# Attention scores in two row halves of TensorE, in two steps a pair, and a new order for the first batch

## The chip, the cores and the metric

The kernel runs on one core of a Trainium2 chip. Its time is the device time of one execution, in microseconds (us). A core has TensorE (matmuls, PE in the profile; PEld is its weight loads), VectorE (DVE), ScalarE (ACT), GpSimd (POOL) and SyncE (SP); SP, POOL and ACT also issue DMA transfers, each in its own queue and in program order. Where a profile row says 128*64, the stationary operand of a matmul has 128 rows (the contraction) and 64 columns.

## The reference

Batch 8, 8 heads, 576 tokens, 64 values a head; 8 token indices are global. All of it in fp32, the kernel's matmuls in bf16.

```python
scores = 0.125 * q @ k.T
mask = (|i - j| <= 32) | is_global[i] | is_global[j]
attn = softmax(where(mask, scores, -1e9))
x = (attn @ v), heads side by side          # 4608 tokens x 512
h = x @ w_in                                # 512 x 2048
g = s * relu(h) ** 2 + b
out = g @ w_out                             # 2048 x 512
```

## The kernel before

**Attention.** The 64 (batch, head) are taken as 32 pairs of heads (p = 0 to 31), four pairs a batch. A pair's K and Q are transposed so that head 0 lies on partitions 0 to 63 and head 1 on 64 to 127. Keys come in five chunks of 128 (120 keys and the 8 global ones), queries in a row of 640 columns, with 8 columns of global queries in each chunk. Chunk c needs only the query columns LO[c] to HI[c]: 160, 192, 192, 192 and 136 of them. Scores come out transposed, keys on partitions and queries on columns.

`qbufs` hold Q as a block diagonal, `[128, 2, 640]`: for head 0 the lower partitions are zero, for head 1 the upper, so that one matmul with all 128 rows of a K chunk gives both heads' scores side by side. A pair has five score steps, `qk(p, c)`, one a chunk, of 2 x 160 to 2 x 192 columns. Each takes a tile of `ps_s` (two buffers of one PSUM bank) and ends in an exponential on ScalarE (L583, L586). For pairs 0 to 4 the mask is added by a matmul of `ident` with a bias table (L573, L579); from pair 5 on VectorE multiplies the exponentials with a 0/1 mask at the next step (L587, through the list `later`).

`pvq(m, blk)` makes the weighted sums of two pairs (m): value rows and a column of ones are stationary, 128x32, four heads in four column groups of the array; query columns are cut in two blocks (0 to 323, 324 to 615) over the five chunks. `norm_steps` divides by the sums: logarithm and negative exponential on ScalarE, then sums and scalings on VectorE into `xt`. `scatter` copies the global tokens' columns into `xt` on POOL, at addresses that POOL has read into registers (`greg_p`, L1008).

**Feed-forward.** `moe_quanta` is a generator: per tile of 512 tokens 16 groups of four matmuls with `win_t` (psh, L698), ReLU on ScalarE, square on VectorE, then 16 groups of four with `wout_t` (pso, L732). `Q()` takes one group ("quantum"), `lead()` one of the two leading pieces of tile 0, which need heads 0 and 1 of `xt` alone.

**Order.** All engines follow the program order written by hand. The first batch (`first_pair`, p = 0 to 4) runs by itself: a table says at which score step which transposes, copies and normalising steps come. Its global K and Q columns come by a matmul with a selection matrix for pairs 0 and 1 (`select`), and from a gather by indirect DMA for the others (`gather(0)`, `globals_of(0)`: `round_g`, `turn`, `move`). Then `run_pair` has eight steps (s) a pair, scores in the first five, and a quantum in nearly each. Q transposes of the next pair stand at s = 5 and use a buffer of `ps_s` too. From pair 8 on K is turned by DMA (`turn_k`, after `round_k`). `cast_v` rounds V into `vring`; `put_v` puts the eight global V rows in.

Of the kernel before, what the change touches and what calls it, by code (L numbers as in the profile page):

```python
# [49 lines left out]
STEP = (CUT, 360)  # L50
MASKED = 1.0e9
# [18 lines left out]
def kernel(  # L70
# [29 lines left out]
    ps_s = ctx.enter_context(tc.tile_pool(name="ps_s", bufs=2, space=bass.MemoryType.PSUM))  # L100
# [52 lines left out]
    qbufs = [const.tile([P, 2, LQ], BF16, name=f"qbd{i}", tag=f"qbd{i}") for i in range(3)]  # L153
    gqd = [const.tile([P, 2, D], BF16, name=f"gqd{i}", tag=f"gqd{i}") for i in range(2)]
# [107 lines left out]
    def clear(ap, n):  # L262
        nc.scalar.copy(out=ap, in_=view(zero[0 : ap.shape[0]], [0, n]))

    onesf = const.tile([P, P], FP32)
    nc.vector.memset(onesf[:], 1.0)
    nc.vector.memset(qbufs[0][0:D, 1], 0.0)
    nc.vector.memset(qbufs[0][D:P, 0], 0.0)
    for t in "kq":
        nc.vector.memset(six[t][NP6:P, 0, :, NJ - 2 :], 0.0)  # L270

    nc.sync.dma_start(
# [20 lines left out]
    for p in range(5):  # L293
        load_v(nc.sync, p)
        if p == 0:
            nc.sync.dma_start(out=sbrow[:, 0:1], in_=_bcast_dram(moe_s[:], 1))
            nc.sync.dma_start(out=sbrow[:, 1:2], in_=_bcast_dram(moe_b[:], 1))
# [34 lines left out]
    def gather(bb, ts="kq"):  # L332
# [26 lines left out]
    iot = const.tile([P, WM], FP32)  # L359
    nc.gpsimd.iota(  # L360
        iot[:, 0:GAP], pattern=[[1, GAP]], base=NG - WIN, channel_multiplier=-1,
        allow_small_or_imprecise_dtypes=True,
    )
    nc.gpsimd.iota(
        iot[:, GAP + NG : WM], pattern=[[1, WM - GAP - NG]], base=HB + NG,
        channel_multiplier=-1, allow_small_or_imprecise_dtypes=True,
    )
    nc.gpsimd.memset(iot[:, GAP : GAP + NG], 100000.0)
    gadd = [const.tile([P, WM], FP32, name=f"gadd{i}", tag=f"gadd{i}") for i in range(2)]
    for t in gadd:  # L370
        nc.gpsimd.memset(t[:], -MASKED)
        nc.gpsimd.memset(t[0:NG, WIN : WIN + P], 0.0)
    band = const.tile([P, WM], FP32)

    def halves(t, eng, h):
# [5 lines left out]
    clear(qbufs[1][0:D, 1], LQ)  # L381
    halves("k", nc.scalar.copy, 1)
    halves("q", nc.scalar.copy, 1)
    nc.scalar.activation(band[:], iot[:], AF.Square)
    nc.gpsimd.tensor_scalar(
        out=band[:], in0=band[:], scalar1=(float(WIN) + 0.5) ** 2, scalar2=MASKED,
        op0=OP.is_le, op1=OP.mult,
    )
    masks, biases = [], []

    def build_biases(cs):
        for c in cs:
            at = sum(W[:c])
            m = wsum[:].bitcast(BF16)[:, at : at + W[c]]
            x0 = LO[c] - P * c + WIN
            nc.vector.scalar_tensor_tensor(
                out=m, in0=band[:, x0 : x0 + W[c]], scalar=notg[:, c : c + 1],
                in1=gadd[c // (NCH - 1)][:, x0 : x0 + W[c]], op0=OP.mult, op1=OP.add,
            )
            biases.append(view(m, [0, 2], [1, W[c]]))  # L400

    def build_masks():
        for c in range(NCH):
            at = sum(W[:c])
            m = const.tile([P, W[c]], BF16, name=f"mask{c}", tag=f"mask{c}")
            nc.vector.tensor_scalar(
                out=m[:], in0=wsum[:].bitcast(BF16)[:, at : at + W[c]],
                scalar1=-0.5, scalar2=None, op0=OP.is_ge,
            )
            masks.append(view(m[:], [0, 2], [1, W[c]]))  # L410
# [17 lines left out]
    def globals_of(bb):  # L428
# [11 lines left out]
        def turn():  # L440
# [7 lines left out]
            def evac():  # L448
                eng = nc.vector.tensor_copy
                eng(out=gkt[bb][:], in_=ps[:, 0])  # L450
                for hh in range(2):
                    r = slice(D * hh, D * hh + D)
                    eng(out=gqd[bb % 2][r, hh], in_=ps[r, 1])
# [26 lines left out]
    def put_kq(p):  # L480
        bb, x = divmod(p, 8)
        eng = A if p < 4 else V
        eng(
            out=view(ktile[p], [P, NCH], [1, NG]),
            in_=view(gkt[bb][:, NG * x : NG * x + NG], [0, NCH], [1, NG]),
        )
        eng(  # L487
            out=view(qbufs[p % 3][:, 0, HB:], [LQ, 2], [P, NCH], [1, NG]),
            in_=view(gqd[bb % 2][:, 0, NG * x :], [D, 2], [0, NCH], [1, NG]),
        )  # L490

    def trans(t, p):
        if p < 5 or (t == "k" and p > 5):
            ps = bank("pst").bitcast(BF16)[:, 0:LQ]
        else:
            ps = ps_s.tile([P, LQ], BF16, tag="s", name="pst")
# [22 lines left out]
    def trans_a(p, later=later):  # L519
# [4 lines left out]
        def evac():  # L524
# [4 lines left out]
            if p == 3:  # L529
                r, n = slice(0, D), HB // NJ  # L530
                nc.vector.tensor_copy(
                    out=view(qbufs[p % 3][r, 0], [P, NCH], [HB + NG, 2], [NJ, n], [1, NJ]),
                    in_=view(qtp[0][r], [2 * n, NCH], [n, 2], [1, n], [NP6, NJ]),
                )
            if 1 < p < 6:
                put_kq(p)
# [3 lines left out]
    qtp = [None]  # L540

    def trans_b(p, later=later):
        ps = qtp[0] = trans("q", p)

        def evac():
            n = HB // NJ
            for hh in (1, 0):
                eng = A if (p, hh) in ((0, 1), (0, 0), (1, 1), (2, 1), (3, 1)) else V
                if eng is V and p == 3:
                    continue  # L550
                r = slice(D * hh, D * hh + D)
                if p >= NSIXQ:
                    eng(  # L553
                        out=view(qbufs[p % 3][r, hh], [P, NCH], [HB + NG, 2], [1, HB]),
                        in_=view(ps[r], [P, NCH], [HB, 2], [1, HB]),
                    )
                    continue
# [622 lines left out]
```

## Time and profile before

| | |
|---|---|
| median of 3 runs | 356.03 us (355.75 to 356.8) |
| profiled execution | 356.0 us, span 354.3 us |
| TensorE busy in the span | 329.9 us (93%) |
| VectorE, ScalarE, POOL busy | 232.7, 219.0, 66.0 us |
| mean granted TensorE clock | 0.981 of full |

The span goes from the first to the last instruction. In a timeline each row is one or more instructions of one line that follow each other: start, duration from the first start to the last end, engine, line, operation, output<-inputs, how many; in brackets how long the engine was idle before, and what ended that. Matmuls are pipelined and their recorded ends include the time to come through, so from one matmul's start to the next one's is the better measure; a few matmul records can be missing. A start in a row can be a little earlier than the end of the row before.

### The profile page before, as it was taken

What the parts mean: (1) busy time and instruction counts of PE and PEld (TensorE: products, weight loads), DVE (VectorE), ACT (ScalarE), POOL (GpSimd) and SP (SyncE); (2) the same over time, 40 slices, a digit from 0 to 9 for tenths busy, and PEclk for the clock granted to TensorE, in tenths of its full rate; (3) what the DMA queues carried; (4) which work ended last, traced back from release to release, by engine and by line L of the source; (5) the groups of instructions that cost most, each with busy time, mean ns of one, the idle gap of its engine ahead of it and who ended that gap; (6) DMA issues with size and microseconds to landing.
All of it is one profiled execution on the core that took longest, in us unless ns stands there. A gap on an engine that the chain in (4) does not pass through costs nothing.

```text
span 354.3 us, 8484 instructions
## 1 busy us (share of the span) xinstructions
PE 329.9 (93%) x3131; PEld 174.0 (49%) x3175; DVE 232.7 (66%) x670; ACT 219.0 (62%) x454; POOL 66.0 (19%) x150
## 2 busy tenths in 40 slices
PE   5868499999999999999999999999999999999996
PEld 3434244454455454557755545544557644444444
DVE  5748367877778888876768686767677644423421
ACT  4647367865987588757876787678747713602610
POOL 5863663005000701030005000300020010000000
PEclk9969879999999999999999999999999999999999
DMA  8999998978997799999189967983440011011002
GB/s 155 222 218 217 208 214 149 187 131 192 208 144 160 171 188 226 206 198 172 23 174 242 208 125 164 247 192 79 150 132 2 2 61 60 1 59 62 0 30 91
DMA packets 122246, 50.23 MB, mean 142 GB/s; under 512 B 108992, under 2 KB 115328, under 8 KB 122196
## 3 DMA queue, kind: packets, MB, share of 16 engines
q1 hardware_dynamic: 113530, 37.84, 53.7%
q0 software_dynamic: 8320, 11.42, 16.1%
q10 hardware_dynamic: 354, 0.43, 0.7%
q8 instruction: 25, 0.41, 0.5%
q14 instruction: 17, 0.14, 0.1%
HBM read 42.35 MB, written 9.44 MB: 146 GB/s over the span
## 4 chain that ended last, share of the span: by engine, by line
PE 77%; DMA 7%; DVE 4%; issue 4%; POOL 3%; ACT 2%; POOLq 1%; SPq 1%; ACTq 0%; DVEq 0%
PE psh L698 32%; PE pso L732 30%; PE pss L574 6%; PE po L604 5%; DMA wst<-in_moe_w_out_dram 3%; DMA natq<-in_q_dram 2%; DMA gf<-in_v_dram,grow 2%; PE pst L499 1%; PE pst L513 1%; POOLq L1008 1%; DVE wsum L1055 1%; PE pss L573 1%; DVE qbd L553 1%; POOL sixk L169 1%; DVE g L723 1%
## 5 line engine op out<-in xcount | busy, mean ns | idle before, releaser
L698 PE MATMUL psh<-xt,win_t 128*128 128x512 bf16 (+4 forms) x685 | 137.3, 342 | 5.5 <-POOL xt L675 4.6
L732 PE MATMUL pso<-wout_t,g 128*128 128x512 bf16 (+1 forms) x569 | 132.9, 373 | 2.1 <-issue 1.4
L720 ACT ACTIVATE r<-psh 128x512 bf16<-128x512 f32 x144 | 86.7, 604 | 58.5 <-PE psh L698 51.3
L698 PEld LDWEIGHTS <-win_t 128*128 128x128 bf16 x704 | 64.2, 98 | 60.5 <-issue 7.7
L732 PEld LDWEIGHTS <-g 128*128 128x128 bf16 x592 | 56.0, 98 | 58.6 <-issue 0.5
L586 ACT ACTIVATE e<-pss 128x384 bf16<-128x384 f32 (+2 forms) x135 | 63.1, 471 | 34.8 <-PE pss L574 32.6
L723 DVE TENSOR_TENSOR g<-r 128x512 bf16<-128x512 bf16 x144 | 59.9, 427 | 37.4 <-ACT r L720 36.4
L587 DVE TENSOR_TENSOR em<-e,mask 128x384 bf16<-128x384 bf16 (+2 forms) x135 | 45.7, 339 | 12.8 <-ACT e L586 11.0
L574 PE MATMUL pss<-qbd,kt 128*128 128x384 bf16 (+2 forms) x160 | 51.0, 322 | 3.2 <-DVE qbd L880 1.5
L675 POOL COPY xt<-xg 128x4 bf16 (+1 forms) x72 | 17.9, 249 | 175.4 <-DVE xt L650 171.6
L752 DVE SCALAR_TENSOR_TENSOR osb<-pso,sb,bias_row 128x512 f32<-128x512 f32 (+1 forms) x25 | 18.1, 726 | 29.7 <-PE pso L732 27.0
L574 PEld LDWEIGHTS <-kt 128*128 128x128 bf16 x160 | 15.8, 99 | 20.2 <-DVE qbd L487 2.7
L650 DVE TENSOR_TENSOR xt<-po,rep 128x480 bf16<-128x480 f32 (+2 forms) x60 | 24.4, 446 | 0.3 <-ACT rep L660 0.3
L553 DVE COPY qbd<-pst 64x600 bf16<-64x600 bf16 x38 | 17.8, 467 | 9.2 <-PE pst L499 8.6
L558 DVE COPY qbd<-pst 64x600 bf16<-64x600 bf16 x20 | 15.6, 780 | 9.8 <-PE pst L513 6.4
L583 ACT ACTIVATE em<-pss 128x384 bf16<-128x384 f32 (+2 forms) x25 | 11.3, 461 | 16.6 <-PE pss L574 13.9
L604 PE MATMUL po<-em,vring 128*32 128x160 bf16 (+3 forms) x840 | 17.1, 218 | 1.1 <-issue 1.1
L205 ACT CAST natb<-natk 128x640 bf16<-128x640 f32 x24 | 17.8, 740 | 0.0
L248 ACT CAST vring<-natv 128x640 bf16<-128x640 f32 x21 | 15.6, 743 | 0.0
L657 ACT ACTIVATE ln<-po 128x324 f32<-128x324 f32 (+1 forms) x30 | 13.1, 437 | 3.8 <-PE po L604 3.7
L660 ACT ACTIVATE rep<-ln 128x324 f32<-128x324 f32 (+1 forms) x32 | 15.3, 477 | 0.1
L229 ACT CAST sixq<-natq 120x640 bf16<-120x640 f32 x19 | 14.3, 755 | 0.0
(137 smaller groups left out, 236.0 us busy)
## 6 DMA issues: line engine op xcount, KB each, us to landing
natv<-in_v_dram SPq DMA_DIRECT2D x57, 150.0 KB
natk<-in_k_dram SPq DMA_DIRECT2D x47, 150.0 KB
out_dram<-osb SPq DMA_DIRECT2D x23, 256.0 KB
natq<-in_q_dram SPq DMA_DIRECT2D x37, 150.0 KB
wst<-in_moe_w_out_dram POOLq DMA_DIRECT2D x8, 512.0 KB
out_dram<-osbh SPq DMA_DIRECT2D x9, 256.0 KB
win_t<-in_moe_w_in_dram POOLq DMA_DIRECT2D x4, 512.0 KB
wout_t<-in_moe_w_out_dram POOLq DMA_DIRECT2D x4, 512.0 KB
```

The lines of the kernel that those rows point to most:

```text
L553: eng(out=view(qbufs[p % 3][r, hh], [P, NCH], [HB + NG, 2], [1, HB]), in_=view(ps[r], [P, NCH], [HB, 2], [1, HB]),)
L574: nc.tensor.matmul(ps[:], ktile[p][:, P * c : P * c + P], qbufs[p % 3][:, :, LO[c] : HI[c]], start=p == 0 or p >= NCH, stop=p > 0,)
L586: nc.scalar.activation(e[:], ps[:], AF.Exp, scale=SCALE)
L587: later.append(lambda: nc.vector.tensor_mul(em[:], e[:], masks[c]))
L604: nc.tensor.matmul(po[DH * j : DH * j + DH, a : a + n], view(vring[:, p % NVR, c, hh, part - 1 :], [2, DH]) if part else onesb[:], emt[(p, ...
L650: nc.vector.tensor_tensor(out=view(xt[:, 2 * g, x0 + t0 :], [NXT, 2], [w, runs], [1, w]), in0=view(po[:, STEP[blk] + col :], [STEP[blk], 2 ...
L675: nc.gpsimd.tensor_copy(out=xt[:, h, S * (bi % NX) : S * (bi % NX) + S][:, :, ds(greg_p[i], 1)], in_=xgs[bi][:, h, i : i + 1],)
L698: nc.tensor.matmul(psh[:, d0 : d0 + n], win_t[:, a, f * P : f * P + P], xt[:, a, x0 : x0 + n], start=(a == 0 and j == 0), stop=(a == 3), s ...
L720: nc.scalar.activation(r[:], psh, AF.Relu)
L723: later.append(lambda g=g, r=r: nc.vector.tensor_mul(g[:], r[:], r[:]))
L732: nc.tensor.matmul(pso[:, 0:nn], gl[f][:, u * P : u * P + P], wout_t[:, f, n0 : n0 + nn], start=(f == 0), stop=(f == 15),)
L752: nc.vector.scalar_tensor_tensor(out=osb[:, 0:nn], in0=pso[:, 0:nn], scalar=s_bc, in1=bias_row[:, n0 : n0 + nn], op0=OP.mult, op1=OP.add,)
```

## The change

Q lies plain in `qbufs`, `[128, 640]`, head 0 on the upper and head 1 on the lower 64 partitions; zeros and their clearing go. A score matmul takes one head: 64 rows of K by 128 keys, against that head's query columns; the two heads alternate and write to two PSUM banks of one tile. The five steps become two, `qk(p, g)`, with the chunk pieces (`PIECES`) that fall in one block of the weighted sums: 160 + 192 + 100 = 452 columns a head, and 92 + 192 + 136 = 420. `ps_s` is one buffer of two banks. In `run_pair` the steps stand at s = 0 and 4 of odd pairs and at 1 and 3 of even ones; `put_out`, the weighted sums, stays at s = 4 of odd and 1 of even pairs.

`first_pair` and its tables are replaced by a straight list. Pairs 0 to 3 take their global K and Q columns by `select`; the gather serves V rows and pairs from 4 on. Some copies of V move from ScalarE to VectorE, the mask band is made on POOL, the scatter of the first batch stands ahead of weight loads on POOL, the register reads come earlier, V of pairs 5 and 6 is loaded from SP's queue.

```diff
+PIECES = []
+for _x0, _x1 in SPAN:          # per block: (chunk, lo, hi, offset)
...
-    ps_s = ctx.enter_context(tc.tile_pool(name="ps_s", bufs=2, ...))
+    ps_s = ctx.enter_context(tc.tile_pool(name="ps_s", bufs=1, ...))
...
-    for p in range(5):
+    load_v(nc.sync, 0)              # ahead of three fills of V's buffers
...
+    for p in range(1, 6):
         load_v(nc.sync, p)
...
-    nc.scalar.activation(band[:], iot[:], AF.Square)
-    nc.gpsimd.tensor_scalar(out=band[:], ...)
+    nc.gpsimd.memset(band[:], MASKED)
+        chop(ap, n, 1, b0 + WIN, -1, 0.0)       # affine_select, four and two more
...
     def trans_b(p, later=later):
-            for hh in (1, 0):
-                eng = A if (p, hh) in (...) else V
-                eng(out=view(qbufs[p % 3][r, hh], ...), in_=view(ps[r], ...))
+            eng = A if p < 4 else V
+            eng(out=view(qbufs[p % 3][:], ...), in_=view(ps, ...))
...
-    def qk(p, c):
-        ps = ps_s.tile([P, 2, W[c]], FP32, tag="s", name="pss")
+    def qk(p, g):
+        ps = ps_s.tile([P, 2, DM], FP32, tag="s", name="pss")
+        def bias(first):
+            for hh in range(2):
+                nc.tensor.matmul(ps[:, hh, 0:n], ident[:], biases[g], ...)
         if 0 < p < NCH:
-            nc.tensor.matmul(ps[:], ident[:], biases[c], start=True, stop=False)
-        nc.tensor.matmul(
-            ps[:], ktile[p][:, P * c : P * c + P], qbufs[p % 3][:, :, LO[c] : HI[c]], ...)
+            bias(True)
+        for c, lo, hi, at in PIECES[g]:
+            for hh in range(2):
+                r = slice(D * hh, D * hh + D)
+                nc.tensor.matmul(
+                    ps[:, hh, at : at + hi - lo], ktile[p][r, P * c : P * c + P],
+                    qbufs[p % 3][r, lo:hi], ...)
...
     def run_pair(p, nq, extra):
+            if p > 4 and s in ((0, 4) if p % 2 else (1, 3)):
+                qk(p, int(s > 1))
             if s < NCH:
-                qk(p, s)
...
-    first_pair(0, {...})
-    load_kq(5); load_v(nc.gpsimd, 5); load_v(nc.gpsimd, 6); load_w_in(1); load_kq(6)
-    greg_p = [...]                  # then load_w_out(0), pairs 1 to 4 by first_pair
+    turned(trans_a, 0)(); q_out = turned(trans_b, 0); select(0)(); q_out()
+    build_biases(0); qk(0, 0); rows_of(0); gather(0, "kqv"); load_kq(4); load_w_in(0)
+    build_biases(1); turned(trans_b, 1)(); qk(0, 1)
+    k_out = turned(trans_a, 1); put = select(1); warm(1); k_out(); put()
+    qk(1, 0); turned(trans_b, 2)(); load_w_in(1); greg_p = [...]; load_kq(5); qk(1, 1)
+    k_out = turned(trans_a, 2); put = select(2); warm(1); k_out(); put(); cast_v(V, 0)
+    qk(2, 0); turned(trans_b, 3)(); cast_v(V, 1); qk(2, 1)
+    k_out = turned(trans_a, 3); put = select(3); k_out(); put()
+    steps0[0](); steps0[2](); flush()               # round_g, move(0)
+    qk(3, 0); put_v(V, 0); put_v(V, 1); steps0[1](); flush()        # turn
+    q_out = turned(trans_b, 4); q_out(); cast_v(A, 2)
+    put_out(0, 0); put_out(0, 1); step(); qk(3, 1); step()
+    k_out = turned(trans_a, 4); step(); step(); flush(); cast_v(V, 3)
+    scatter(0, 0); load_w_out(0); load_kq(6); put_v(V, 2); put_v(V, 3)
+    put_out(1, 0); put_out(1, 1); k_out(); step(); step(); flush(); step(); step()
+    qk(4, 0); flush(); steps0[3](); flush(); scatter(0, 1); load_w_out(1)
+    load_v(nc.sync, 6); load_nat(nc.sync, "k", 8); load_v(nc.sync, 7); load_q(8)
+    cast_v(A, 4); qk(4, 1); lead(); load_kq(7); load_w_out(2)
...
+    q_out = turned(trans_b, 5); k_out = turned(trans_a, 5); q_out(); k_out(); lead()
...
+                if j == 12:                         # loads of K and Q of pair 12
+                    at(4, load_nat, nc.sync, "k", j); at(4, load_q, j)
...
+        if p == 6:                                  # were at 1 and 3
+            at(4, round_k, 8); at(6, turn_k, 8)
+        if p == 7:                                  # was at 3 of pair 6
+            at(2, round_q, 8)
```

Lines of the diff that follow each other without more are put in one row here.

## Rows read from the trace of the kernel before

**Rows 1.** Busy time by engine in three stretches (columns: stretch, then each engine, clock, DMA).

```profile
40.00:45.00 5.00, 2.03 (x6) 0.70 (x7) 0.41 (x4) 0.00 (x0) 4.01 (x18) 0.61 1.25 229
45.00:50.00 5.00, 5.00 (x39) 2.65 (x39) 3.27 (x8) 3.11 (x7) 4.39 (x7) 0.71 1.21 217
...
180.00:200.00 20.00, 19.74 (x182) 9.82 (x187) 15.74 (x45) 13.02 (x28) 5.18 (x11) 1.00 0.96 220
```

**Rows 2.** Timeline of TensorE over one pair of heads.

```profile
189.90 0.30 PE L574 MATMUL pss<-qbd,kt 128*128 128x320 bf16 x1
...
190.90 0.33 PE L574 MATMUL pss<-qbd,kt 128*128 128x384 bf16 x1
191.06 1.03 PE L732 MATMUL pso<-wout_t,g 128*128 128x512 bf16 x4
...
193.98 0.28 PE L574 MATMUL pss<-qbd,kt 128*128 128x272 bf16 x1
194.19 0.38 PE L604 MATMUL po<-em,onesb 128*32 128x160 bf16 x12
...
194.90 0.82 PE L698 MATMUL psh<-xt,win_t 128*128 128x512 bf16 x3
...
196.03 2.75 PE L698 MATMUL psh<-xt,win_t 128*128 128x512 bf16 x12
198.62 0.30 PE L574 MATMUL pss<-qbd,kt 128*128 128x320 bf16 x1
```

**Rows 3.** Timeline of TensorE, two places where the stationary shape changes.

```profile
52.74 0.45 PE L513 MATMUL pst<-ident,sixk 96*64 96x96 bf16 x12
53.12 0.38 PE L604 MATMUL po<-em,onesb 128*32 128x160 bf16 x12
...
69.07 0.33 PE L574 MATMUL pss<-qbd,kt 128*128 128x384 bf16 x1
69.33 0.25 PE L446 MATMUL psg<-ident,gb 64*64 64x64 bf16 x4
69.51 0.82 PE L732 MATMUL pso<-wout_t,g 128*128 128x512 bf16 x3
```

**Rows 4.** Timeline of TensorE, six transposes in a row and what follows.

```profile
88.76 0.42 PE L507 MATMUL pst<-ident,sixq 96*128 96x96 bf16 x6
89.02 2.75 PE L698 MATMUL psh<-xt,win_t 128*128 128x512 bf16 x12
```

**Rows 5.** Timeline of all engines, the exponential of the score step at 193.98.

```profile
194.67 0.39 ACT L586 ACTIVATE e<-pss 128x272 bf16<-128x272 f32 x1
```

**Rows 6.** Groups by line and shape (count, then busy us, mean ns, idle before).

```profile
L586 ACT ACTIVATE e<-pss 128x384 bf16<-128x384 f32 x81 | 40.3, 499 | 15.5 <-PE pss L574 13.2 <-DVE em L587 1.7 <-issue 0.5
...
L586 ACT ACTIVATE e<-pss 128x272 bf16<-128x272 f32 x27 | 11.3, 419 | 0.6 <-PE pss L574 0.6
...
L525 DVE COPY kt<-pst 128x600 bf16<-128x600 bf16 x8 | 6.2, 775 | 3.3 <-PE pst L513 3.0 <-PE pss L574 0.3
```

**Rows 7.** Timeline of all engines, the first batch.

```profile
10.76 0.44 ACT L583 ACTIVATE em<-pss 128x320 bf16<-128x320 f32 x1 [0.63 <-PE pss L579]
...
21.25 0.26 DVE L438 CAST gb<-gf 128x192 bf16<-128x192 f32 x1 [4.25 <-DMA gf<-in_v_dram,grow]
...
27.45 0.38 PE L604 MATMUL po<-em,onesb 128*32 128x160 bf16 x12
...
33.47 0.38 PE L604 MATMUL po<-em,onesb 128*32 128x160 bf16 x12
...
38.84 0.79 DVE L650 TENSOR_TENSOR xt<-psx,rep 128x480 bf16<-128x480 f32 x2
...
40.71 3.89 POOL L675 COPY xt<-xg 128x2 bf16 x16
...
42.75 0.59 PE L698 MATMUL psh<-xt,win_t 128*128 128x512 bf16 x1 [4.57 <-POOL xt L675]
...
46.18 3.17 PE L698 MATMUL psh<-xt,win_t 128*128 128x512 bf16 x10
```

More of the change, by code (lines that the diff above doesn't have):

```diff
@@ L50 @@
 STEP = (CUT, 360)
+PIECES = []
+for _x0, _x1 in SPAN:
+    _at, _ps = 0, []
+    for _c in range(NCH):
+        _lo, _hi = max(LO[_c], _x0), min(HI[_c], _x1)
+        if _lo < _hi:
+            _ps.append((_c, _lo, _hi, _at))
+            _at += _hi - _lo
+    PIECES.append(_ps)
+GW = [_ps[-1][3] + _ps[-1][2] - _ps[-1][1] for _ps in PIECES]
 MASKED = 1.0e9
@@ L450, in evac @@
                 eng(out=gkt[bb][:], in_=ps[:, 0])
[L451 to L453 removed]
+                eng(out=gqt[bb % 2][:], in_=ps[:, 1])
             later.append(evac)
@@ L614, in pvq @@
                     lo += n
+                    at += n
     def norm_steps(m, blk):
@@ L1009 @@
     ]
[L1010 removed]
+    load_kq(5)
+    qk(1, 1)
+    k_out = turned(trans_a, 2)
+    put = select(2)
+    warm(1)
+    k_out()
+    put()
+    cast_v(V, 0)
+    qk(2, 0)
+    turned(trans_b, 3)()
+    cast_v(V, 1)
+    qk(2, 1)
+    k_out = turned(trans_a, 3)
+    put = select(3)
+    k_out()
+    put()
+    steps0[0]()
+    steps0[2]()
+    flush()
+    qk(3, 0)
+    put_v(V, 0)
+    put_v(V, 1)
+    steps0[1]()
+    flush()
+    q_out = turned(trans_b, 4)
+    q_out()
+    cast_v(A, 2)
+    put_out(0, 0)
+    put_out(0, 1)
+    step()
+    qk(3, 1)
+    step()
+    k_out = turned(trans_a, 4)
+    step()
+    step()
+    flush()
+    cast_v(V, 3)
+    scatter(0, 0)
+    load_w_out(0)
+    load_kq(6)
+    put_v(V, 2)
+    put_v(V, 3)
+    put_out(1, 0)
+    put_out(1, 1)
+    k_out()
+    step()
+    step()
+    flush()
+    step()
+    step()
+    open_batch(1)
+    qk(4, 0)
+    flush()
+    steps0[3]()
+    flush()
+    scatter(0, 1)
+    load_w_out(1)
+    load_v(nc.sync, 6)
     load_nat(nc.sync, "k", 8)
+    load_v(nc.sync, 7)
     load_q(8)
[L1013 to L1032 removed]
+    cast_v(A, 4)
+    qk(4, 1)
+    lead()
+    load_kq(7)
+    load_w_out(2)
     first.close()
[L1034 removed]
+    ps_n = ctx.enter_context(tc.tile_pool(name="ps_n", bufs=2, space=bass.MemoryType.PSUM))
+    rings.append(ps_n)
     turns[0] = 5
[L1036 to L1037 removed]
+    q_out = turned(trans_b, 5)
+    k_out = turned(trans_a, 5)
+    q_out()
+    k_out()
     lead()
[L1039 to L1040 removed]
     for i in (1, 2, 3):
```

315 lines of the change are left out of this document (112 added, 203 removed).

## Prediction, made before the changed kernel ran

> **What bounds the kernel now.** I read the table of stretches first. In the long middle (180 to 200 us) TensorE is busy 19.74 of 20 us at the full granted clock while VectorE has 15.74 and ScalarE 13.02 [rows 1]: TensorE is the limit there, and work taken from the other two buys nothing by itself. In the first 50 us it is different: from 40 to 45 us TensorE is busy 2.03 of 5 us, its granted clock falls to 0.61, and it is still 0.71 in the next five [rows 1]. So the time is the date at which TensorE starts its unbroken stream of feed-forward matmuls, plus what that stream contains.
>
> TensorE's timeline of one head pair shows the stream [rows 2]. A pair starts at 189.90 and the next at 198.62: 8.72 us. Twelve 512-column matmuls take 198.62 - 196.03 = 2.59 us, 0.216 each, or 2,370 columns per us. A 384-column score matmul takes 191.06 - 190.90 = 0.16 us, so nothing but its columns. The five score steps hold 320 + 3 x 384 + 272 = 1,744 columns, 0.736 us a pair. For the first batch I read all engines' timelines for the dates of its milestones [rows 7].
>
> **The change in the steady pairs.** Each head's scores now use 64 rows of the array, 872 columns for each head, and the two heads' matmuls alternate. If the halves work at the same time, that is 872 columns, 0.368 us: 0.368 saved a pair, 9.9 us over the 27 pairs after the first five. No row of before shows two 64-row, 128-column matmuls, so this is bounded from both sides: side by side (0.368 us) or one after another (0.736, nothing saved). The nearest row is the four 64x64 transposes at 69.33, too short to tell, and the twelve 64-column transposes at 52.74, whose two column halves do go side by side (next work starts after 0.38 us, while 12 x 96 columns in a row would need 0.49) [rows 3]. I take side by side.
>
> Against this stands the price of leaving the 128x128 shape. The scores before stay in the shape of the feed-forward matmuls; the new ones don't. The weighted sums (128x32) show what a visit costs: the last score matmul starts at 193.98 and needs 0.115, the sums start at 194.19 (0.095 later) and the next feed-forward matmul at 194.90; four column groups side by side stream 3 x 452 columns in 0.572, so the visit costs 0.81 - 0.57 = 0.233 us beside its columns [rows 2]. The 64x64 visit costs about the same: 69.07 + 0.162 to 69.51 is 0.278 us for 128 columns, 0.054 side by side, so 0.224 [rows 3]. Between two other shapes, 52.74 + 0.243 to 53.12, it is 0.137 [rows 3]. In the new order one score step of a pair stands alone (0.233) and the other is followed at once by a block of weighted sums: 0.095 in, 0.137 between, and the 0.095 that the sums paid already, so 0.137 more. Together 0.37 us a pair. Bounds: nothing (a change of rows alone costs no wait) to 0.37.
>
> The Trainium skill (TensorEngine Tiling (Array Packing), Key Properties) says that changing the tiling mode drains TensorE while changing the tile within a mode does not. The rows of both other shapes agree, at 0.22 to 0.23 us a visit; by the rule a pair gains 0.368 and pays 0.37, by the column count alone it gains 0.368.
>
> So a pair comes out even: 0.368 - 0.37 = 0.00, with ends of -9.9 us (free visits) and +10.0 us (halves in turn, 27 x 0.37).
>
> Smaller terms. Weight loads go from 5 to 12 a pair. Six transposes with a 128-column load each take 89.02 - 88.76 = 0.26 us, so a load needs at most 0.043 [rows 4]; six in a row at that price last 0.26 against the step's 0.19 and 0.18 of columns: 0.15 us a pair at most, 4.0 us in all, 0 at least. I take 0.02, or 0.5 us, since 0.24 of the 0.26 is columns. The two exponentials read 904 and 840 values: from 499 ns for 384 and 419 for 272 [rows 6], 0.71 ns a value, some 0.87 and 0.82 us, against 2.34 for the five; VectorE's mask products go from five to two, the copy of Q into place from two to one, and the copies of the global columns get smaller. All this is on engines that have 4 to 7 us in 20 to spare [rows 1]: 0 us. If TensorE waited for them it would show there.
>
> The score buffer becomes one tile of two banks where there were two tiles. A score step, or the Q transposes that share the buffer, must wait for the exponential before it. In even pairs two groups of feed-forward matmuls (2 x 0.864) cover it. In odd pairs the last step is followed by sums and one group, 0.81 + 0.86 = 1.67 us, and then the transposes. Behind them wait all further TensorE work. The present last exponential starts 194.67 - 194.10 = 0.57 us after its matmul, since a ReLU stands before it [rows 2, 5]; 0.57 + 0.82 = 1.39 is hidden by 0.3. One more such delay ahead of it would uncover 0.3: 13 odd pairs, 0 to 4 us. I take 0.
>
> The loads moved (V of pair 0 ahead of the fills; V of 5 and 6 from POOL's queue to SP's; the K and Q loads of 12, and the rounding and DMA transpose of K of 8, two or three steps later) keep the bytes and have pairs of 8.72 us to land in: 0, with a K transpose late for pair 8 (about 1 us) as the price if not.
>
> **The change in the first batch.** Before, the milestones are [rows 7]: first exponential 10.76; the gathered globals land and are rounded at 21.25; first weighted sums 27.45, those of pairs 2 and 3 33.47; last normalised block 38.84 + 0.79 = 39.63; POOL, behind its weight loads, starts the scatter at 40.71, 16 copies in 3.89 us; TensorE's first feed-forward matmul at 42.75, after 4.57 us idle, and at half the rate (ten from 46.18 last 3.17 us). The eight leading half-groups (f of 0 to 3, heads 0 and 1) are through four matmuls after 46.18, at 47.9.
>
> After: the globals of pairs 1 to 3 come by a selection matmul, so their scores no longer wait for the gather. The mask band is made by selects on POOL in place of a square on ScalarE that waited for a cast there; it has until 9.7 us, so 0. The bias table's first group is three pieces on VectorE ahead of the first exponential; I put that at 11.4, 0.6 later. With one score buffer a pair is a chain, from second step to second step: transposes 0.5, the K copy 0.78 [rows 6], two small copies of the globals (half of that, 0.4), scores 0.36, an exponential 0.9, bias and scores 0.74 (0.38 + 0.19, and 0.17 to come through). That is 3.7, with little waits 4.0 us at full clock, 4.9 at half. From 13.2 (end of the second step of pair 0) two pairs, then K and globals of pair 3, 1.7, make 22.9 (25.5 at half clock). The gathered V rows then need 0.27 to round [rows 7], a pass through TensorE and three copies, 2.0 by the K copy: first sums at 25.2 (27.9), 27.45 before. Up to the sums of pairs 2 and 3 there are 6.0 us now [rows 7]; into that chain come pair 3's second score step with its exponential, ahead of the first reciprocal (0.4 + 0.9), and a V cast on VectorE (0.78), so 8.1: 33.3. TensorE is nearly idle from 28 to 33, and I count what follows at half clock, as after the idle stretch at 40 us before [rows 1]: the sums to 36.0 (two blocks of 1.35), pair 4's scores to 39.5 (twice 1.3, and 0.9 between), eight half-groups of 0.43 and pair 5's transposes (1.2) to 44.2.
>
> On POOL the first half of the scatter now stands ahead of the weight loads and the second ahead of all but one, so it is through at about 40.8 and TensorE never waits for it. What is late next: K and Q of pairs 6 and 7 and three quarters of w_out are now behind VectorE's last scaling; by the dates above they are issued by 43 us, and w_out is used only after sixteen groups of feed-forward matmuls (16 x 0.86 = 13.8 us), so 0, with 1 to 2 us as the price if DMA lags. So 44.2 against 47.9: 3.7 us earlier. All at full clock it would be 40.5 (7.4 earlier), all at half 46.5 (1.4 earlier); 0 if the longer VectorE row loses that too.
>
> **The sum.** Profiled execution: 356.0 us, with a span of 354.3 and 1.7 outside; the runs' median is 356.03, so no correction. 354.3 - 3.7 + 0.0 + 0.5 = 351.1, and 352.8 with the 1.7.
>
> **The rivals.**
> *The visits are cheap.* Rows alone change, the columns stay 128 wide, and the array needs no wait. Nothing in the trace speaks against it directly; the two shapes that it shows both split columns. Then 9.9 us go as well: 342.9. Half of the price gives 347.8.
>
> *The halves take turns, slower.* One mechanism, in every score step from pair 5 on: the second head's matmul starts when the first's ends. Then a pair pays 0.37 for nothing, 10.0 us: 362.8. It decides against the change once the overlap saves less than 0.37 - 3.7/27 = 0.23 us a pair. The column halves at 52.74 speak against it. The Trainium skill (TensorE: Matmul & The Clock Gate, Part 3: Packing small matmuls) has matmuls in different row groups overlap; no row of before shows it.
>
> *The first batch gains nothing.* One score buffer, and normalisation in one long VectorE row, eat what the POOL queue and the gather gave. Then 354.3 + 0.5 + 1.7 = 356.5. The 6.0 against 8.1 us speaks for it, the 4.57 us idle before the first feed-forward matmul against it.
>
> **How the numbers follow.** My forecast (even pairs, earlier start, 349 to 355.5) 0.45; cheap visits (341 to 349) 0.22; no gain in the first batch (355.5 to 358) 0.17; halves in turn, or the single buffer's stalls (358 to 364) 0.16. A measurement of this kernel tells about 0.3% (1.1 us) from no change. Faster takes the first two cases, 0.67, less 0.03 for a start that comes to little: 0.64. Same: the 0.03 and 0.10 of the third case: 0.13. Slower: 0.07 and 0.16: 0.23. The range leaves out one in ten at either end: 343 (half of the cheap visits) to 360 (most of the turns). The forecast's own range is 349 to 355.5.
>
> **What would show it.** Right: a lone score step takes some 0.42 us from the end of the matmul before to the next feed-forward matmul (0.19 columns, 0.23 visit), pairs still take 8.7 us, the half-groups are through near 44. Cheap visits: pairs of 8.35 us. Turns: second-half matmuls start as the first's end, and pairs take 9.1. Stalls: TensorE's transposes wait for the exponential in odd pairs. Wrong start: first feed-forward matmul at 42 or later, and VectorE the last releaser before it.

## The result, and the profile after

The changed kernel takes **350.87 us** (median of 20 runs, 350.25 to 354.58) where the kernel before took 355.99 in runs beside it: a ratio of 0.9885, 95% interval 0.9861 to 0.9909. Its times lie in two groups, 350.3 to 351.4 and 353.0 to 354.6. The profiled execution is of the first: 350.42 us, a span of 348.7 and 1.7 outside. The prediction was 352.8 us, with 343 to 360 as its range. Each ratio in this text leaves out executions more than 1.5% above the fastest of their kernel (two of nine in e10, two of twelve in e9), while the medians are over all.

First TensorE's timeline over two pairs of the changed kernel, which answers to [rows 2]:

```profile
184.70 0.37 PE L583 MATMUL pss<-qt,kt 64*128 64x160 bf16 x6
185.00 1.90 PE L742 MATMUL pso<-wout_t,g 128*128 128x512 bf16 x7
...
188.56 0.36 PE L583 MATMUL pss<-qt,kt 64*128 64x92 bf16 x6
188.85 0.39 PE L613 MATMUL po<-em,onesb 128*32 128x160 bf16 x12
...
195.24 1.90 PE L708 MATMUL psh<-xt,win_t 128*128 128x512 bf16 x7
197.07 0.36 PE L583 MATMUL pss<-qt,kt 64*128 64x92 bf16 x6
197.36 1.90 PE L708 MATMUL psh<-xt,win_t 128*128 128x512 bf16 x8
...
202.05 0.37 PE L583 MATMUL pss<-qt,kt 64*128 64x160 bf16 x6
```

Two pairs take 202.05 - 184.70 = 17.35 us, 8.68 each. An even and an odd pair of the kernel before, up to 198.62 in [rows 2], start here:

```profile
181.21 0.30 PE L574 MATMUL pss<-qbd,kt 128*128 128x320 bf16 x1
```

That is 17.41 us for two (the 8.72 of the prediction was the longer one), so a pair gets 0.03 us shorter. The lone step at 197.07 shows the price of a visit: eight 512-column matmuls from 195.24 (one has no record) need 8 x 0.216 = 1.73, so 0.10 passes before the step starts; the step has 420 columns (0.177) and the next matmul follows after 0.29, so 0.11 more. The step at 188.56, with the weighted sums right behind it, also takes 0.29: 0.11 above its columns. So a pair pays 0.21 + 0.11 = 0.32 to 0.33 for the visits and saves 0.368 of columns, 0.04 in all.

The stretches answer to [rows 1] (columns as there):

```profile
34.00:36.00 2.00, 0.56 (x12) 0.26 (x12) 1.90 (x8) 0.28 (x1) 0.21 (x1) 0.59 0.56 111
36.00:38.00 2.00, 1.37 (x44) 1.16 (x48) 1.78 (x6) 0.01 (x1) 1.52 (x8) 0.50 0.58 132
38.00:40.00 2.00, 2.00 (x40) 1.01 (x34) 1.23 (x5) 1.76 (x4) 1.94 (x3) 0.50 1.00 253
40.00:42.00 2.00, 1.50 (x22) 0.76 (x17) 1.82 (x6) 1.54 (x2) 0.60 (x4) 0.71 0.80 134
42.00:44.00 2.00, 1.95 (x33) 1.11 (x31) 0.43 (x1) 1.48 (x2) 1.57 (x7) 1.00 1.06 165
180.00:200.00 20.00, 19.74 (x195) 9.62 (x195) 14.05 (x37) 13.93 (x24) 5.40 (x11) 1.00 1.12 210
```

In the middle TensorE is busy 19.74 of 20 us, as before, while VectorE falls from 15.74 to 14.05. ScalarE shows more in this window (13.93 for 13.02), but over the whole span it falls from 219.0 to 205.4. In the first batch TensorE again stands, but for one group of sums, now from 32.4 to 36.5 us, and its granted clock is then 0.50 (1.2 GHz) until about 41. For the time up to 30.9 us the trace has no clock record and the profile prints 1.00, but matmuls run there as at 0.50: the bias's two matmuls of 452 columns take 0.89 us at 20.41 and 0.87 at 38.87, where 0.50 is on record, and its two of 420 columns 0.45 at 31.22. In the kernel before, record and full rate begin at 13.8 us. The timeline of all engines over the first batch answers to [rows 7]:

```profile
16.56 0.92 ACT L593 ACTIVATE em<-pss 128x904 bf16<-128x904 f32 x1 [2.65 <-PE pss L583]
...
20.33 0.19 DVE L875 CAST qt<-psg 128x40 bf16<-128x40 f32 x1
20.41 0.96 PE L573 MATMUL pss<-wsum,ident 128*128 128x452 bf16 x2 [0.33 <-issue]
...
21.30 0.56 PE L583 MATMUL pss<-qt,kt 64*128 64x160 bf16 x6
...
21.90 0.92 ACT L593 ACTIVATE em<-pss 128x904 bf16<-128x904 f32 x1 [2.13 <-PE pss L583]
...
25.78 0.25 DVE L450 CAST gb<-gf 128x192 bf16<-128x192 f32 x1
...
28.82 0.57 PE L613 MATMUL po<-em,onesb 128*32 128x160 bf16 x12
...
34.29 0.56 PE L613 MATMUL po<-em,onesb 128*32 128x160 bf16 x12 [1.89 <-ACT rep L670]
...
35.79 2.16 POOL L685 COPY xt<-xg 128x2 bf16 x8 [8.69 <-DVE xt L660]
...
36.56 1.25 PE L613 MATMUL po<-em,vring 128*32 128x160 bf16 x26 [1.71 <-DVE vring L485]
...
41.37 1.97 POOL L685 COPY xt<-xg 128x2 bf16 x8 [1.27 <-DVE xt L660]
...
42.05 1.04 PE L708 MATMUL psh<-xt,win_t 128*128 128x512 bf16 x3
...
45.09 1.89 PE L708 MATMUL psh<-xt,win_t 128*128 128x512 bf16 x8 [0.76 <-DVE kt L534]
```

The first weighted sums are later than before (28.82, against 27.45), those of pairs 2 and 3 as well (34.29, and their V part 36.56, against 33.47). What is won comes after them: no wait for POOL, and pair 4's scores done before the feed-forward work. The eight half-groups are through two matmuls after 45.09, at 45.5; before it was 47.9. From the first feed-forward matmul to there it is 3.47 us at a granted clock of 1.00; before it was 5.15 us (42.75 to 47.9) at 0.50. So 1.7 of these 2.4 us lie in that stretch.

The rest is in the waits of TensorE from 50 to 160 us. Before, by what it waited for (us in total, times, longest):

```profile
PE pss L574 <- DVE qbd L487: 0.8, 2, 0.6
...
PE pss L574 <- ACT e L586: 0.6, 2, 0.4
PE po L604 <- DVE xt L650: 0.6, 1, 0.6
```

After, the same stretch and view:

```profile
PE pst L516 <- ACT e L596: 0.7, 1, 0.7
```

So 2.0 us of waits for ScalarE and VectorE became 0.7.

TensorE's timeline shows two dates by which the rest is read, the first output matmul and the sixth return from output to input matmuls. After:

```profile
63.02 1.25 PE L742 MATMUL pso<-wout_t,g 128*128 128x512 bf16 x5
...
256.40 1.91 PE L708 MATMUL psh<-xt,win_t 128*128 128x384 bf16 x16
```

Before:

```profile
66.81 0.38 PE L732 MATMUL pso<-wout_t,g 128*128 128x512 bf16 x1
...
262.24 1.04 PE L698 MATMUL psh<-xt,win_t 128*128 128x384 bf16 x8
```

Stage by stage, changed kernel against the kernel before (starts on TensorE): half-groups through 45.5 against 47.9 (-2.4); first output matmul 63.02 against 66.81 (-3.8, so -1.4 here, of which 0.40, 0.61 and 0.20 are waits of before); the third return from output to input matmuls 151.03 against 156.03 (-5.0, so -1.2, one 0.57 wait among it); the sixth 256.40 against 262.24 (-5.8, so -0.8); end 348.7 against 354.3 (-5.6, so 0.2 is lost again).

### The profile page after: what moved, and what is told of

It is laid out like the page before. It is cut to its first block, busy times and chain, and to the rows that moved or that the text cites. A ratio compares the mean times of both kernels' runs of the same rounds, so it can differ in the third digit from the quotient of the medians.

```text
span 348.7 us, 8756 instructions
## 1 busy us (share of the span) xinstructions
PE 328.8 (94%) x3393; PEld 171.3 (49%) x3439; DVE 207.1 (59%) x544; ACT 205.4 (59%) x347; POOL 64.5 (18%) x156
## 4 chain that ended last, share of the span: by engine, by line
PE 89%; DVE 3%; issue 3%; ACT 3%; DMA 1%; ACTq 0%; DVEq 0%
PE psh L708 35%; PE pso L742 35%; PE po L613 6%; PE pss L583 5%; PE pss L573 2%; PE pst L508 1%; PE pst L522 1%; DMA natq<-in_q_dram 1%; ACT em L593 1%; DVE xt L660 1%; DVE kt L534 1%; PE psg L866 1%; PE pst L516 0%; ACT sixq L244 0%; ACT vring L258 0%
## 5 line engine op out<-in xcount | busy, mean ns | idle before, releaser
L708 PE MATMUL psh<-xt,win_t 128*128 128x512 bf16 (+4 forms) x684 | 132.1, 340 | 2.3 <-issue 0.8
L742 PE MATMUL pso<-wout_t,g 128*128 128x512 bf16 (+1 forms) x568 | 129.2, 373 | 2.6 <-issue 2.1
L596 ACT ACTIVATE e<-pss 128x904 bf16<-128x904 f32 (+1 forms) x54 | 48.4, 896 | 32.0 <-PE pss L583 32.0
L597 DVE TENSOR_TENSOR em<-e,mask 128x904 bf16<-128x904 bf16 (+1 forms) x54 | 33.8, 627 | 26.4 <-ACT e L596 26.3
L583 PE MATMUL pss<-qt,kt 64*128 64x192 bf16 (+4 forms) x384 | 24.7, 240 | 0.8 <-DVE qt L875 0.4
L583 PEld LDWEIGHTS <-kt 64*128 64x128 bf16 x384 | 11.5, 99 | 27.2 <-issue 17.0
L593 ACT ACTIVATE em<-pss 128x904 bf16<-128x904 f32 (+1 forms) x10 | 9.0, 897 | 16.0 <-PE pss L583 7.2
L550 DVE COPY qt<-pst 128x600 bf16<-128x600 bf16 x19 | 8.9, 468 | 12.1 <-PE pst L508 12.1
L613 PEld LDWEIGHTS <-vring 128*32 128x32 bf16 x896 | 14.6, 102 | 2.3 <-DVE vring L485 2.3
L613 PE MATMUL po<-em,onesb 128*32 128x192 bf16 (+2 forms) x360 | 11.7, 238 | 2.0 <-ACT rep L670 1.9
## 6 DMA issues: line engine op xcount, KB each, us to landing
win_t<-in_moe_w_in_dram POOLq DMA_DIRECT2D x4, 512.0 KB, 13.8
wout_t<-in_moe_w_out_dram POOLq DMA_DIRECT2D x4, 512.0 KB, 13.8
```

The source lines that it names most:

```text
L583: nc.tensor.matmul(ps[:, hh, at : at + hi - lo], ktile[p][r, P * c : P * c + P], qbufs[p % 3][r, lo:hi], start=at == 0 and not 0 < p < NCH ...
L596: nc.scalar.activation(e, ps[:, :, 0:n], AF.Exp, scale=SCALE)
L597: later.append(lambda: nc.vector.tensor_mul(em[:], e, masks[g]))
L613: nc.tensor.matmul(po[DH * j : DH * j + DH, a : a + n], view(vring[:, p % NVR, c, hh, part - 1 :], [2, DH]) if part else onesb[:], emt[(p, ...
L708: nc.tensor.matmul(psh[:, d0 : d0 + n], win_t[:, a, f * P : f * P + P], xt[:, a, x0 : x0 + n], start=(a == 0 and j == 0), stop=(a == 3), s ...
L742: nc.tensor.matmul(pso[:, 0:nn], gl[f][:, u * P : u * P + P], wout_t[:, f, n0 : n0 + nn], start=(f == 0), stop=(f == 15),)
```

## The experiments

The median and the times of each are beside runs of the kernel before on the same chip; ratios are to those. Since the times of one kernel spread over 4 us, the steady stage is compared by the distance, in the profile, from the first output matmul to the sixth return to input matmuls: 193.38 us in the changed kernel, 195.43 before.

**e0_same**: no edit.

> The changed kernel again, unedited. Its 20 times lie in two groups, near 350.6 and near 354. If the two come from the first batch (how long TensorE stays at half clock there), a profile of the slower group has the same distance between first and later feed-forward phases as the faster one and differs before 63 us only; if they come from the steady pairs, that distance (193.4 us from the first pso matmul to the psh matmuls at 256.4) is longer.

352.11 us (350.24 to 354.25, 8 runs), ratio 0.9898 (0.9861 to 0.9934), span 348.9, distance 193.38. The spread of the times is the kernel's own; the distance repeats. Without any edit the median is 1.2 us above the first one, so a difference of that size between the medians below tells nothing.

**e1_full_rows**: score matmuls from pair 5 on use 128 rows (each sums both heads).

```diff
-                r = slice(D * hh, D * hh + D)
+                r = slice(D * hh, D * hh + D) if by_pe else slice(0, P)
```

> From pair 5 on each score matmul takes all 128 rows of K and Q instead of one head's 64 (so it sums both heads' scores, and the output is not the reference's); count, columns, buffers, order as in the changed kernel. Theory (a pair gains 0.368 us of columns and pays 0.33 for the visits to the 64-row shape): a pair gets 0.04 us longer, 0.9 us over the 22 pairs between the first pso matmul and the psh matmuls at 256.4, so that distance goes from 193.4 to 194.3 and the time up by about 1.1 us. Rival (visits are nearly free, the halved columns are the gain): 0.3 us a pair, distance 200, time up by 8 to 10 us. Rival (halves take turns): no gain of columns to lose, the visits are saved: distance 186, time down by 8.

354.75 us (352.06 to 355.38), ratio 0.9962 (0.9934 to 0.9990); distance 194.76, 1.38 more. Its TensorE timeline:

```profile
187.78 0.56 PE L583 MATMUL pss<-qt,kt 128*128 128x160 bf16 x6
188.17 1.89 PE L742 MATMUL pso<-wout_t,g 128*128 128x512 bf16 x7
...
191.62 0.53 PE L583 MATMUL pss<-qt,kt 128*128 128x92 bf16 x6
192.08 0.38 PE L613 MATMUL po<-em,onesb 128*32 128x160 bf16 x12
```

The lone step has 904 columns, 0.381 us, and the next feed-forward matmul follows after 0.39: with 128 rows there is no price for the visit. Ahead of the sums (840 columns, 0.354) it is 0.46, the 0.11 that the sums pay themselves. So twice the columns with no visits cost almost what half the columns with visits do: halves and visits are both real, and nearly cancel. The weight loads are twelve a pair here too, and the lone step takes 0.01 more than its columns. Of the 3.8 us by which the profiled execution is longer than the changed kernel's, 2.3 lie ahead of the first output matmul (65.28 for 63.02), in a part that the edit leaves as it is.

**e2_heads_in_turn**: in a step the three matmuls of one head, then the three of the other.

```diff
+        if not by_pe:
+            pairs = [(x, hh) for hh in range(2) for x in PIECES[g]]
```

> From pair 5 on all pieces of head 0 come first, then all of head 1; same matmuls. Theory (halves overlap only if matmuls of different halves follow each other): step 1 needs 147 + 188 ns of columns instead of 188 and step 2 120 + 177 instead of 177, since only the last piece of head 0 overlaps with head 1; 0.27 us a pair, 6 us in the 22 pairs (193.4 to 199.3), 7 us in all. Rival (halves overlap in any order, or never): 0.

351.89 us (350.68 to 354.79), ratio 0.9898 (0.9866 to 0.9930), distance 193.67 (+0.29).

```profile
197.21 0.36 PE L586 MATMUL pss<-qt,kt 64*128 64x92 bf16 x6
197.51 1.90 PE L711 MATMUL psh<-xt,win_t 128*128 128x512 bf16 x8
```

The step still takes 0.30 us, where 840 columns one after another would need 0.354 beside the visit's 0.11. The expected +6 us did not come: my reading, that only alternating heads lets the halves overlap, is wrong here. Three matmuls of one half and three of the other overlap as well.

**e3_steps_apart**: the second score step of a pair is moved away from the block of weighted sums.

```diff
-            if p > 4 and s in ((0, 4) if p % 2 else (1, 3)):
+            if p > 4 and s in (0, 3):
```

> From pair 5 on the score steps stand at s = 0 and 3 of every pair, so that none is followed at once by weighted sums: both are lone visits. Theory (every change of shape costs about 0.1 us): the step that was chained pays one more change, 0.10 us a pair, 2.2 us in the 22 pairs (193.4 to 195.6) and 2.7 in all. Rival (a visit of 64 rows by 128 columns costs nothing by itself): 0. Rival (the single score buffer stalls the transposes in odd pairs now): a gain of up to 2 us, since the exponential then has two groups more.

352.43 us (351.99 to 352.83), ratio 0.9889 (0.9848 to 0.9930), distance 195.69, 2.31 more, as expected from 0.10 more a pair. The step now stands alone:

```profile
189.06 0.36 PE L583 MATMUL pss<-qt,kt 64*128 64x92 bf16 x6
189.34 1.04 PE L708 MATMUL psh<-xt,win_t 128*128 128x512 bf16 x4
...
190.31 0.39 PE L613 MATMUL po<-em,onesb 128*32 128x160 bf16 x12
```

That a step stands next to the sums is thus worth 0.10 us a pair, the entry of one visit.

**e4_scatter_late**: on POOL both halves of the scatter behind the loads of pair 7 and the second piece of the output weights.

```diff
-    scatter(0, 0)
...
-    scatter(0, 1)
     load_w_out(1)
+    load_kq(7)
+    scatter(0, 0)
+    scatter(0, 1)
```

> Both halves of the first batch's scatter stand behind the weight and K/Q loads on POOL again and run together, as in the kernel before. Theory (POOL's order is one reason for the earlier start): 16 copies of 0.25 us begin at 41.4 us, the eight that the first feed-forward matmul needs end at 43.4 instead of long before, the rest at 45.4: first psh matmul at 43.4 for 42.05, first pso matmul 1.3 to 2 us later than 63.0. Rival (the start hangs on VectorE and ScalarE alone): nothing, since the second half ended at 43.3 anyway.

350.92 us (350.53 to 351.37), ratio 0.9860 (0.9841 to 0.9880). The copies run when they did:

```profile
35.90 2.16 POOL L685 COPY xt<-xg 128x2 bf16 x8 [1.27 <-DVE xt L660]
41.47 1.97 POOL L685 COPY xt<-xg 128x2 bf16 x8 [3.42 <-DVE xt L660]
```

They wait for VectorE; the order of POOL's queue, which the prediction had as what lets the stream start earlier, changes nothing (first output matmul at 63.13). The two halves still run apart, each behind its own data, so what their being split is worth was not tested.

**e6_gather_for_2_3**: pairs 2 and 3 take their global columns from the gather again, not from the selection matmul.

```diff
-    put = select(2)
...
-    put()
+    steps0[0]()
+    steps0[1]()
+    flush()
+    put_kq(2)
```

> Pairs 2 and 3 take their global K and Q columns from the gather again, not by the selection matmul. Theory (the gather's landing held up the first batch before: TensorE waited 3.5 us for it): the third gather lands at 21 to 21.5, then rounding, transposes and two copies put pair 2's first scores at 23 instead of 21.3, and all that follows 1 to 2 us later; two selections of 24 matmuls are saved, 0.3 us each. Rival (with the rest of the new order the gather has landed in time): 0 or a gain of 0.5 us.

351.98 us (350.14 to 353.57), ratio 0.9901 (0.9874 to 0.9927).

```profile
27.32 0.38 PE L613 MATMUL po<-em,onesb 128*32 128x160 bf16 x12
...
32.53 0.38 PE L613 MATMUL po<-em,onesb 128*32 128x160 bf16 x12 [1.89 <-ACT rep L670]
34.80 1.25 PE L613 MATMUL po<-em,vring 128*32 128x160 bf16 x26 [1.89 <-DVE vring L485]
```

The sums are 1.5 us earlier without the selection: the gather had landed anyway, against the expectation. But the end of the batch hardly moves, with the first output matmul at 62.83 against 63.02; the granted clock is 0.50 until 43.6 us here, for 41.2 in the changed kernel, and may have taken the gain.

**e5_v_rows_early** and **e8_both**: the gathered V rows of pairs 2 and 3 put into place ahead of the normalisation of pairs 0 and 1; in e8 also pair 5's K copy ahead of its Q copy. **e12_k_first** has the second edit alone.

```diff
-    flush()
     cast_v(V, 3)
+    put_v(V, 2)
+    put_v(V, 3)
+    flush()
...
     k_out = turned(trans_a, 5)
-    q_out()
     k_out()
+    q_out()
```

> The V cast of pair 3 and the global V rows of pairs 2 and 3 go on VectorE before the sums and scalings of pairs 0 and 1, not behind them. Theory (the long VectorE row holds up the sums of pairs 2 and 3: they start at 34.3 and then wait to 36.56 for the V rows): they run through from about 34.3, so everything after comes 1.5 to 2 us earlier, first pso matmul at 61 to 61.5, and with a shorter idle stretch the half clock between 34 and 41 us may not come: up to 2 us more, 347 to 349 us, and the slower group of times (354) gets rarer. Rival (ScalarE's logarithms and reciprocals set the pace there): less than 0.5 us.

> The order of e5 and, for pair 5, the K copy before the Q copy. Theory (a leading group of feed-forward matmuls waits 0.8 us for the bank that the K transposes hold until their copy): 0.5 to 0.8 us less than e5. Rival (pair 5's first scores then wait for Q instead): as e5.

> Only the copies of pair 5 change places: the K copy before the Q copy, and the V rows stay where the changed kernel has them. Theory: the stream of half-groups waits for the K copy (0.76 us at 45.09) and begins earlier by the time of the Q copy, 0.5 to 0.8 us: first expert output at about 62.4, median 350.3. Rival: the earlier V rows and this swap only help together, since alone each leaves the other's wait in place: first expert output at 63, median 351.

e5 takes 351.08 us (349.99 to 351.61), ratio 0.9860 (0.9838 to 0.9882); the stream starts at 43.88, but the first output matmul, expected at 61 to 61.5, is at 62.35, only 0.67 earlier, and later on it loses 1.3 us (below). e8 takes **349.54** (348.42 to 350.76), ratio 0.9829 (0.9808 to 0.9850). This interval alone lies wholly below the changed kernel's (0.9861 to 0.9909). e12 alone takes 351.89 (349.73 to 354.14), ratio 0.9896 (0.9860 to 0.9932): nothing. In its profile the first output matmul is at 64.57, later than both expectations, with a granted clock of 0.50 until 45.4 us. e8's stretches and TensorE rows:

```profile
34.00:36.00 2.00, 0.79 (x40) 0.59 (x40) 1.90 (x8) 1.03 (x4) 0.00 (x0) 1.00 0.91 187
36.00:38.00 2.00, 1.86 (x56) 1.19 (x57) 1.97 (x9) 1.48 (x4) 1.47 (x8) 1.00 0.97 215
```

```profile
34.81 0.58 PE L613 MATMUL po<-em,vring 128*32 128x160 bf16 x28
...
42.04 1.89 PE L708 MATMUL psh<-xt,win_t 128*128 128x512 bf16 x8 [0.33 <-DVE kt L534]
```

The V part of the sums no longer waits (34.81 for 36.56), the clock stays at 1.00, the stream starts 3 us earlier and the first output matmul is at 60.12 (-2.9). This execution is the fastest of e8's five and the only one with a mean clock of 1.00 (the others have 0.994 or 0.995). In e5's, with the same V rows, the V part starts at 35.19 and the clock is 0.50 from 36.2 to 39.6 all the same. So how much of the 2.9 is the clock's is not shown. The kernel keeps 2.0 us in its span and 1.3 in its median: VectorE now waits 1.96 us, until 62.13, for the gathered rows of the second batch to land, and the stage from 60.12 to the next input matmuls takes 0.8 us longer than in the changed kernel.

**e10_warm**: fourteen matmuls on zeros fill TensorE's stand. **e11_warm_both**: the same with e8's edits. **e9_all_three**: e8's edits with e6's.

```diff
     k_out = turned(trans_a, 4)
+    psw = ps_m.tile([P, DM], FP32, tag="moe", name="psw")[:]
+    for _ in range(14):
+        nc.tensor.matmul(psw, dummy[:, 0:P], dummy[:])
```

> Fourteen matmuls on zeros (512 columns each, about 3.0 us at full clock) are put into the stretch from 32.4 to 36.5 us in which TensorE of the changed kernel stands, ahead of the sums of pairs 2 and 3; nothing else is altered. Theory: the granted clock of 0.50 from about 34.8 to 41.4 us follows that stand; with TensorE busy through it the windows there show 1.00, the sums of pairs 2 and 3 and the scores of pair 4 take half as long as in the changed kernel (0.57 instead of 1.25 us for the second block), the first expert output begins 1 to 2.5 us earlier (60.5 to 62), and the times of the kernel no longer reach 353 to 354: median 349 to 350.3. Rival: the engines that feed TensorE there (the copies on VectorE) set the end of the batch and the clock costs nothing: first expert output at 63, median 351 as the changed kernel.

> V rows early and K copy of pair 5 first, with the fourteen matmuls on zeros at the same place as well. Theory: the V rows have already shortened the stand so far that the clock holds at 1.00, so the matmuls have nothing to give and stand in the way by up to 1 us: median 349.5 to 350.5. Rival: in some executions of the kernel without them the clock still falls, and its times (348.4 to 350.8) close up at their lower end: median 348.5 to 349.

> V rows early, K copy of pair 5 first, and the gather instead of the selection for pairs 2 and 3, all three. Theory: the 1.5 us that the selection costs ahead of the first sums is passed on once the stand at 32 to 36 us is gone: first expert output at 58.6 to 59.5 (60.1 with the first two alone), median 348 to 349. Rival: the next thing that is late, the second batch's own gather and exponentials (0.4 and 0.7 us of waits at 62 to 65 us with the first two), takes it: median 349.5 as with the first two.

e10 takes 354.45 us (350.07 to 356.11, 9 runs), ratio 0.9918 (0.9884 to 0.9951); e11 352.95 (350.95 to 354.10), 0.9916 (0.9884 to 0.9949); e9 352.33 (348.84 to 355.56, 12 runs), 0.9890 (0.9860 to 0.9920). All three came out above what either side had expected. In e10 the granted clock is 1.00 in every stretch from 32 to 48 us, and the first output matmul is at 62.84, for 63.02 in the changed kernel: holding the clock gained 0.2 us. The batch before the stand ran about 0.8 us later in this execution, so the clock may have given that much back. The times spread as widely as ever: four of e11's six executions have a mean granted clock of 1.00, and they go from 350.95 to 354.10. So the half clock alone doesn't make the spread. e10's profile (354.84 us) shows what it loses instead, in a row of VectorE's timeline and in the waits of TensorE from 130 to 158 us:

```profile
140.95 0.69 DVE L1045 TENSOR_TENSOR wsum<-wsum,wst 128x512 f32<-128x512 f32 x1 [4.42 <-DMA wst<-in_moe_w_out_dram]
```

```profile
PE po L613 <- DVE xt L660: 1.7, 1, 1.7
PE pss L583 <- DVE qt L493: 0.9, 1, 0.9
```

VectorE sums the rows of the output weights for the bias and works in order: while one 512 KB piece is late, the Q copy, the mask product and the scaling of the next pairs stand behind it, and TensorE behind them. The piece was issued at 132.88 here and at 132.81 in the changed kernel; it took 8.0 us to land for 4.0 there. So it was not issued late, and no run shows why it took longer. Behind TensorE's stand the granted clock falls too, to 0.69 in the stretch from 145 to 150 us. From its third run of output matmuls to the return to input matmuls (133.47 to 155.44) e10 takes 21.97 us, the changed kernel 17.63 (133.40 to 151.03).

The same row, VectorE's longest single wait for this DMA between 56 and 160 us, over the profiles: under 0.1 us in e3; 0.2 to 0.4 in the changed kernel, e0, e1, e2, e4, e6 and e12; 1.8 in e8, 2.3 in e11, 2.6 in e9, 3.0 in e5, 4.4 in e10. What TensorE lost in that stage goes with it: nothing up to 0.4; 1.3 in e5, 0.9 in e9, 2.5 in e11 and 4.3 in e10, while e8's 1.8 stayed covered. e11 also loses 2.75 us in the stage before, where VectorE waits 3.44 us for the second batch's gather. e9's profiled execution (349.04) is among its fastest, so what makes its median 352.33 is not in it.

## Why the prediction was right, and where its steps were off

**The steady pairs: right, even to the size.** The forecast was 0.368 of columns saved and 0.37 of visits paid; measured are 0.368 and 0.32 to 0.33, and a pair gets 0.03 to 0.04 shorter. The lone visit is 0.21 (forecast 0.233), the chained one 0.11 (0.137). e1 shows both parts at once, and e3 that the entry costs 0.10. The rule cited from the Trainium skill (TensorEngine Tiling (Array Packing), Key Properties), that a change of tiling mode drains TensorE, agrees with those numbers: the change costs, and with 128 rows (e1) the step lasts its columns. Weight loads, forecast at 0.5 us, cost nothing that shows: e1 has as many, and 0.01 us a step beside its columns. The rival of cheap visits (342.9) is out by the 0.21, the rival of halves in turn (362.8) by the 0.29 us a step, and its overlap doesn't even need the alternating order (e2).

**The first batch: earlier, as forecast, but by less and on another path.** The forecast was -3.7 by the half-groups; measured is -2.4 there. The step that was off is the chain up to the first sums: they were to come at 25.2 (27.9 at half clock), and came at 28.82. A pair took 21.90 - 16.56 = 5.34 us, where 4.0 were forecast and 4.9 at half clock. TensorE did run at half its rate, until 30.9 us. Besides, it works the bias in ahead of both steps of a pair, and the chain of the forecast had it ahead of the second only: the copies that pair 2's first scores need are done at 20.52, but the bias matmuls keep TensorE until 21.30.

From the first sums on the legs were forecast well: 7.74 us to the V part of pairs 2 and 3 (forecast 8.1), 2.31 for those sums (2.7), 3.18 for pair 4's scores (3.5). The half-groups took 3.47 for 4.7, since the clock was 1.00 there and not 0.50. The two reasons that the prediction gave for the earlier start, the selection and POOL's queue, are not what makes it: without either (e6, e4) the first output matmul comes as early. It had not seen that the V part of pairs 2 and 3 waits for V rows behind the normalisation on VectorE (1.71 us); with these moved ahead and the K copy (e8) the stream begins 3 us earlier. What does bring the start forward against the kernel before was not separated further by a run: scores, exponentials and normalisation went to fewer, longer instructions in the same edit as the order. The half clock, for which 1.4 to 7.4 us stood in the bounds, was worth about 1.0 us at most where it lasts until 41 (e10: 0.2 and 0.8).

**The savings of ScalarE and VectorE: put at 0, worth 1.3 us or so.** I had judged them by the middle of the kernel, where both engines have time to spare. Between 50 and 160 us TensorE of the kernel before waits 2.0 us for them, for exponentials, copies of the global Q columns and a normalised block; 0.7 is left. This is read from the traces; no run takes these savings away by themselves. The time of the exponential was forecast well (0.87 and 0.82 for the two; measured 0.92 and 0.87):

```profile
L596 ACT ACTIVATE e<-pss 128x904 bf16<-128x904 f32 x27 | 24.9, 922 | 26.9 <-PE pss L583 26.9
L596 ACT ACTIVATE e<-pss 128x840 bf16<-128x840 f32 x27 | 23.5, 869 | 5.0 <-PE pss L583 5.0
```

**The single score buffer: right at 0** in the odd pairs. One transposition waits for an exponential in the whole steady stage, 0.7 us in the second batch. The moved loads cost nothing that shows in TensorE's waits, as forecast.

So the sum: forecast -3.7 + 0.0 + 0.5 = -3.2 of span, measured -5.6. It is made of -2.4 for the start (forecast -3.7), about -1.3 for the waits (0), -0.8 to -1.1 for 27 pairs at 0.03 to 0.04 (0.0), nothing for the weight loads (+0.5), and 0.8 to 1.1 more that no row gives a name to. Part of that may be the waits again, since the view counts from the recorded end of the matmul before: the stage with the wait of 0.57 (137.58 to 156.03) takes 0.76 longer than the like one without it (209.50 to 227.19). That the start fell 1.3 us short and the waits, put at 0, gave 1.3 back is luck.

**What stays open.** No profile shows an execution of the changed kernel's second group of times. Their mean granted clock is 0.984 or 0.985, that of the first group 0.989 to 0.995, so half clock lasts longer in them. The profiles of e1 and e12 show such cases: 0.50 until 46.2 and 45.4 us, and the first output matmul at 65.28 and 64.57, 2.3 and 1.5 us later than in the changed kernel. If the second group is like them, that accounts for 1.5 to 2.3 of the 3 us between the groups. But e6's profiled execution, also at 0.984, took 350.14, and e10 shows that a late weight piece can make up as much by itself. No run that only moves the weight pieces was made, so that they cause the losses of e5, e9, e10 and e11 is read from the traces, not shown by an edit.

## What to carry to other kernels

Price a change of the array's shape by the visit, not by the matmul: some 0.1 us in and 0.1 out, so put visits of different shapes side by side, and count the columns saved against the visits made. Before costing a saving on an engine at nothing, list the bound engine's waits in every stage and not in the middle alone. An earlier start is kept only as far as the next transfer is early too: look up which DMA, and which in-order queue behind it, the new date will meet.

## What the runs showed of the hardware that I had not expected

- Matmuls in different row halves overlap when three of one half are issued ahead of three of the other: 0.30 us for the step, as when they alternate (e2).
- Up to the first clock record of a trace the profile prints a granted clock of 1.00, but TensorE works at half its later rate, as at 0.50 (1.2 GHz). In each profile the rate doubles where the record begins: at 13.8 us in the kernel before, 30.9 in the changed one, 26.6 in e6, 32.0 in e10. So the clock of the first stretches has to be read from the matmuls, and the mean clocks of whole executions leave that part out.
- Fourteen matmuls on zeros kept the granted clock at 1.00 through a stand of 4 us behind which it is 0.50 for 6.8 us without them (e10), and the first output matmul came 0.2 us earlier. With the V rows moved (e8, e5) it stayed at 1.00 in the one profile and was 0.50 for 3.4 us in the other.
